# One overlapping request for x in both halves, earlier stores of a weight combination, and a new order in the first section and at the end

## The chip, the core and the metric

The kernel runs on one core of one Trainium2 chip. What counts is the device time of one execution in microseconds; the figure used is the median of several executions. TensorE (PE) multiplies, VectorE (DVE), ScalarE (ACT) and GpSimd (POOL) do the elementwise work, and SyncE (SP) issues the transfers (DMA) between the memory of the chip (DRAM) and the on-chip buffer of 128 partitions. Results of PE land in PSUM.

## What is computed

S = 2048 rows of D = 576 values; 32 heads of 18 values each; the feed-forward part has F = 4608 columns.

```python
def _A_ref(x, wqkv, wo):                      # attention, H = 32, Dh = 18
    qkv = (x @ wqkv).reshape(B, S, 3, H, Dh).transpose(2, 0, 3, 1, 4)
    ...
    p = softmax(einsum("bhqd,bhkd->bhqk", q, k) * (Dh ** -0.5))
    o = einsum("bhqk,bhkd->bhqd", p, v)
    return o.transpose(0, 2, 1, 3).reshape(B, S, D) @ wo

def _B_ref(x, w_gate, w_up, w_down):          # feed-forward
    return (gelu(x @ w_gate) * (x @ w_up)) @ w_down

xn = layernorm(x)
return x + _A_ref(xn, ...) * silu(_B_ref(xn, ...))
```

All of it is float32. The large products are made from high and low parts (hi = rounded, lo = raw - hi) in three terms: hi hi, lo hi, hi lo.

## The kernel before

**Stages.** The prologue normalises x, transposes it (x transposed, xn, called x below), splits it into a high part (xth) and a low part (xtl), stores both in the DRAM tensors xhs[b], one for each block b of TB = 512 rows, and makes Q, K and V. There a scheduler orders ACT, DVE and SP. Behind it PE's order is written out by hand: 144 sections of gate and up (4 blocks b, 18 row groups r of w_down, two sections g in each), between whose matmuls stand the matmuls of the attention, and after each two sections the product with w_down. At the end come the last sections and the projection of the attention's output, in 128-row groups, each called a step.

**A section** (section, gate_up) makes 128 columns of gate (pg) and of up (pu) for the 512 rows of the block. The 576 values of the contraction are 9 chunks of 64. Gate's chunk lies on the partitions 0 to 63, up's on 64 to 127, and the two matmuls of a pair run on the two halves of PE; a section has 27 pairs (9 chunks, three terms). So x has to lie in both halves: xd is three tiles (k = 0, 1, 2) of three chunks each, each with a high and a low tile, 128x3x512. The weights come by load_gu in two requests, one for each half (64x9x128 of w_gate, the same of w_up), and split_gu makes high parts (wh) and low parts (wl) of three chunks at a time. The weights of the next section are split in the section before: the first two thirds at its start, the last behind its pairs.

**The passage to the next block.** In the last section of a block (n + 1 divisible by 36) the x of the next block is loaded: load_xd hooks the tiles 0 and 1 behind the pairs 9 and 18 and loads tile 2 at the end. A request fills the partitions 0 to 63 only (halves = 1); copy_xd then copies the high tiles on ACT and the low tiles on POOL to the partitions 64 to 127. The tile 2 comes by two requests for each part instead (halves = 2). There are three passages, from block 0 to 1, 1 to 2 and 2 to 3; the first block's x (XD) is loaded in the prologue and copied by POOL.

**Attention between the pairs.** A slot makes scores (pm, max_pair) for the maximum on DVE, then scores (pe, score_pair), their exponential pT on ACT, and the values (acc). pm, pe, acc, py of w_down and the end's po share a ring of three PSUM slots (ring, RING = 3): PE waits where the reader of an older slot is late.

**w_down** (down) takes seven products of combined quarters of h (ah, al) and of the weights (T); DVE adds them into M. T is formed in the first blocks from raw rows (rawd; cut_plain_b, high_b, low_b) and for the groups in FORMED stored to the DRAM tensor ts (t_piece with store), to be loaded again later. The pieces of a group are stored at hooks, i.e. behind numbered pairs of the next section: 13 and 20 for the high pieces, 2 and 9 of the section after for the low.

**The end.** step() is one group of 128 rows: project (po from oh, ol and the output weights woh, wol), multiply (yy), between() (work put in here, as last_down), finish_rows (the sum into xx or xxs, and its store), and split_o(k + 2), which makes the high part oh on ACT and the low part ol on DVE of the group after the next. last_section makes the last gate and up sections, in PSUM of their own ("f") or in the ring ("ring"). ACT, DVE and POOL have the order of the program text here.

The line that fills the lower half, and the copy to the upper:

```python
nc.sync.dma_start(f(t)[HR * a:HR * a + HR],
                  xhs[b][i, k * XG * HR:(k + 1) * XG * HR, :].rearrange("(k p) t -> p k t", p=HR))
...
keep(nc.scalar.activation(x[0][HR:P, i], f(x[0])[0:HR, i], AF.Copy))
```

## Time and profile before

| what | before |
| --- | --- |
| median of three runs | 2551.31 us (2550.46 to 2553.19) |
| the profiled execution | 2552.37 us |
| its span | 2550.6 us |
| instructions | 52903 |
| granted TensorE clock | 1.00 |
| bytes moved, mean rate | 446.88 MB, 175 GB/s |
| ACT and POOL busy | 1461.7 us (57%), 1639.3 us (64%) |

The times are those of the device; the profile is of one execution, and its span leaves out what lies before the first and behind the last instruction. A row of the timeline reads: start in us from the span's start, duration in us, engine, line of the kernel, operation, output tile <- input tiles, shape, and how many instructions stand in the row; in brackets the idle time of the engine before it and the instruction that ended it. SPq is SP as the issuer of transfers, so that its duration is that of the issue and not of the transfer. PEld is the loading of weights into PE, which runs beside its matmuls.

### The profile page before, as it was taken

What the parts mean: (1) busy time and instruction counts of PE and PEld (TensorE: products, weight loads), DVE (VectorE), ACT (ScalarE), POOL (GpSimd) and SP (SyncE); (2) the same over time, 40 slices, a digit from 0 to 9 for tenths busy, and PEclk for the clock granted to TensorE, in tenths of its full rate; (3) what the DMA queues carried; (4) which work ended last, traced back from release to release, by engine and by line L of the source; (5) the groups of instructions that cost most, each with busy time, mean ns of one, the idle gap of its engine ahead of it and who ended that gap; (6) DMA issues with size and microseconds to landing.
All of it is one profiled execution on the core that took longest, in us unless ns stands there. A gap on an engine that the chain in (4) does not pass through costs nothing.

```text
span 2550.6 us, 52903 instructions
## 1 busy us (share of the span) xinstructions
PE 2537.9 (100%) x20548; PEld 1835.7 (72%) x20548; DVE 2092.3 (82%) x2371; ACT 1461.7 (57%) x1765; POOL 1639.3 (64%) x1708
## 2 busy tenths in 40 slices
PE   9999999999999999999999999999999999999999
PEld 8888866666766676666667666776666677666688
DVE  5327888889888888888887888998888888889367
ACT  3223466666666665555666555655556665556621
POOL 3105688888888875656658555666667666666773
PEclk9999999999999999999999999999999999999999
DMA  8855465555685566667787767766668666665775
GB/s 262 272 187 136 117 175 164 156 165 163 169 215 157 162 174 147 166 165 165 170 191 188 174 166 169 170 169 169 154 160 207 162 173 172 164 170 151 190 209 213
DMA packets 410321, 446.88 MB, mean 175 GB/s; under 512 B 107092, under 2 KB 287060, under 8 KB 410072
## 3 DMA queue, kind: packets, MB, share of 16 engines
q1 hardware_dynamic: 410072, 443.50, 65.7%
q8 instruction: 164, 2.69, 0.5%
q14 instruction: 85, 0.70, 0.1%
HBM read 347.30 MB, written 96.08 MB: 174 GB/s over the span
## 4 chain that ended last, share of the span: by engine, by line
PE 98%; DVE 1%; ACT 0%; DMA 0%; issue 0%; POOL 0%; SPq 0%; DVEq 0%
PE pg L431 24%; PE acc L887 18%; PE py L547 15%; PE pu L431 11%; PE pm L824 9%; PE pe L870 9%; PE po L200 6%; PE po L1041 2%; PE pgu L431 2%; PE py L534 1%; PE pt L270 0%; DVE KA L771 0%; DMA xx<-in_A_x_dram 0%; DMA KA<-qk 0%; ACT pT L871 0%
## 5 line engine op out<-in xcount | busy, mean ns | idle before, releaser
L871 ACT ACTIVATE pT<-pe 128x1024 f32<-128x1024 f32 x1024 | 1047.3, 1027 | 580.5 <-PE pe L870 547.6
L825 DVE TENSOR_REDUCE mx<-pm 128x2 f32<-128x1024 f32 x1024 | 1221.1, 1224 | 164.9 <-PE pm L824 148.3
L431 PE MATMUL pu<-xd,wh 64*128 64x512 f32 x2466 | 901.7, 396 | 0.0
L431 PE MATMUL pg<-xd,wh 64*128 64x512 f32 x2466 | 901.6, 396 | 0.0
L431 PEld LDWEIGHTS pg<-xd,wh 64*128 64x128 f32 x2466 | 454.6, 184 | 111.6 <-issue 53.9
L431 PE MATMUL pu<-xd,wl 64*128 64x512 f32 x1233 | 481.9, 391 | 0.0
L431 PE MATMUL pg<-xd,wl 64*128 64x512 f32 x1233 | 481.8, 391 | 0.0
L431 PEld LDWEIGHTS pu<-xd,wh 64*128 64x128 f32 x2466 | 454.6, 184 | 22.4 <-ACT xd L160 0.2
L887 PE MATMUL acc<-pT,VS 128*32 128x512 f32 x4096 | 466.0, 595 | 0.0
L117 POOL TENSOR_SCALAR wh<-raw 128x384 fp32r<-128x384 f32 x402 | 217.2, 542 | 370.4 <-PE pu L431 264.8
L119 POOL TENSOR_TENSOR wl<-raw,wh 128x384 fp32r<-128x384 f32 x402 | 415.8, 1036 | 28.4
L824 PE MATMUL pm<-KA,QT 64*128 64x512 f32 x2048 | 411.7, 394 | 3.0 <-ACT pT L871 2.7
L870 PE MATMUL pe<-QT,KA 64*128 64x512 f32 x2048 | 410.1, 392 | 0.0
L547 PE MATMUL py<-T,ah 128*128 128x288 f32 x1876 | 380.9, 298 | 0.0
L554 DVE TENSOR_TENSOR M<-py,M 128x576 f32<-128x576 f32 x448 | 339.4, 757 | 32.0 <-PE py L547 18.0
L547 PEld LDWEIGHTS py<-T,ah 128*128 128x128 f32 x1876 | 298.8, 188 | 54.0 <-issue 54.0
L460 POOL TENSOR_TENSOR al<-h,ah 128x512 fp32r<-128x512 f32 (+1 forms) x143 | 295.6, 2067 | 59.8 <-ACT ah L457 50.0
L887 PEld LDWEIGHTS acc<-pT,VS 128*32 128x32 f32 x4096 | 120.1, 109 | 276.6 <-issue 229.7
L547 PE MATMUL py<-T,al 128*128 128x288 f32 x938 | 276.1, 294 | 0.0
L870 PEld LDWEIGHTS pe<-QT,KA 64*128 64x128 f32 x2048 | 192.8, 184 | 109.4 <-DVE mx L825 24.3
L431 PEld LDWEIGHTS pg<-xd,wl 64*128 64x128 f32 x1233 | 227.4, 184 | 31.9 <-POOL wl L124 0.3
L431 PEld LDWEIGHTS pu<-xd,wl 64*128 64x128 f32 x1233 | 227.3, 184 | 11.9
(170 smaller groups left out, 2968.6 us busy)
## 6 DMA issues: line engine op xcount, KB each, us to landing
T<-ts SPq DMA_DIRECT2D x98, 576.0 KB
KA<-qk SPq DMA_DIRECT2D x768, 72.0 KB
T<-ts SPq DMA_DIRECT2D x98, 432.0 KB
raw<-in_B_w_gate_dram SPq DMA_DIRECT2D x144, 288.0 KB
raw<-in_B_w_up_dram SPq DMA_DIRECT2D x144, 288.0 KB
ts<-T SPq DMA_DIRECT2D x36, 576.0 KB
VS<-vs SPq DMA_DIRECT2D x128, 152.0 KB
qk<-t SPq DMA_DIRECT2D x72, 256.0 KB
```

Source lines behind the costliest of these rows:

```text
L117: first = nc.gpsimd.tensor_scalar(hi, raw, 1.0, 1.0, op0=ALU.mult, op1=ALU.mult)
L119: keep(nc.gpsimd.tensor_tensor(lo, raw, f(hi), op=ALU.subtract))
L200: nc.tensor.matmul(o, st, m, start=(i == 0), stop=(i == len(terms) - 1))
L431: nc.tensor.matmul(o, w[1 + wp][k][rr, c, :], xd[k][xp][rr, c, :], start=(i == 0), stop=(i == len(terms) - 1))
L460: low = two.tensor_tensor(lo, raw, f(hi), op=ALU.subtract)
L547: nc.tensor.matmul(py[:, t, 0:DC], h[:, i, tt], T[:, w, k], start=n == 0, stop=n == 2)
L554: nc.vector.tensor_tensor(M[:, m], py[:, :, 0:DC], M[:, m], op=ALU.add)
L824: nc.tensor.matmul(pm[:, a], QS[u, r][rr, t * P:(t + 1) * P], KS[(u * NA + c) % KB][r][rr, :], start=True, stop=True)
L825: nc.vector.tensor_reduce(MX[u][:, 2 * r:2 * r + 2, t, c], pm, axis=AX.X, op=ALU.max)
L870: nc.tensor.matmul(pe[:, a], KS[(u * NA + c) % KB][r][rr, t * P:(t + 1) * P], QS[u, r][rr, :], start=True, stop=True)
L871: nc.scalar.activation(PT[u, kt][:, 2 * r:2 * r + 2, :], pe, AF.Exp, scale=SCALE)
L887: nc.tensor.matmul(ACC[u][32 * a:32 * a + 32, :], VS[(u * NA + c) % VB][:, v:v + 32], pt[:, a, :], start=first, stop=last, skip_group_chec ...
```

## The change

Five things are changed.

1. xhs[b] has 64 more rows, a repetition of the first 64 of its block, written by two more stores in the prologue. load_xd makes one request of 128 partitions for each tile, in which partition p reads row 192 k + 64 c + p for c = 0, 1, 2: the partitions 64 to 127 read the rows that lie 64 further on. The upper half so holds each chunk's successor, and the copies on ACT and POOL are gone, those of the prologue too.
2. load_gu loads w_up shifted to match: chunks 1 to 8 in one request, chunk 0 in another at the end. A section has three weight requests in place of two.
3. The high pieces of the combination that is formed last before the passage from block 0 (`late`) are stored at the hooks 1 and 3 rather than 13 and 20.
4. In section 0, T's cut (cut_plain_b) stands behind the third split of the next weights.
5. At the end, step() splits o (split_o) before between() and finish_rows; the last section (first + 4) follows the section in the ring directly, its weights are loaded before the loads of T that follow, and split in two pieces ahead of the sums of h and one behind.

```diff
--- before.py
+++ after.py
@@ -105,7 +105,7 @@
     ys = dram.tile([S - TB, D], F32, name="ys")
     zeros = dram.tile([2, 2 * TB], F32, name="zeros")
     ts = dram.tile([NR, P, 2 * 7 * DC], F32, name="ts")
-    xhs = [dram.tile([2, D, TB], F32, name=f"xhs{b}") for b in range(NB)]
+    xhs = [dram.tile([2, D + HR, TB], F32, name=f"xhs{b}") for b in range(NB)]
 
     ident = const.tile([P, P], F32, name="ident")
     make_identity(nc, ident)
@@ -133,8 +133,9 @@
     def load_gu(t, keep=lambda i: i):
 
         raw = raw_tile([P, NC, P])
-        for a, w in enumerate((w_gate, w_up)):
-            keep(nc.sync.dma_start(raw[HR * a:HR * a + HR], w[:, t * P:(t + 1) * P].rearrange("(k p) n -> p k n", p=HR)))
+        cols = slice(t * P, (t + 1) * P)
+        for to, rows in ((raw[0:HR], w_gate[:, cols]), (raw[HR:P, 0:NC - 1], w_up[HR:D, cols]), (raw[HR:P, NC - 1:NC], w_up[0:HR, cols])):
+            keep(nc.sync.dma_start(to, rows.rearrange("(k p) n -> p k n", p=HR)))
         return raw, [], []
 
     def split_gu(w, k, cut=split):
@@ -143,24 +144,16 @@
         w[1].append(hi)
         w[2].append(lo)
 
-    def load_xd(b, k, halves=1):
+    def load_xd(b, k):
 
         out = []
         for i in range(2):
             t = wts.tile([P, XG, TB], F32R, name=f"xd{i}_{k}")
-            for a in range(halves):
-                nc.sync.dma_start(f(t)[HR * a:HR * a + HR],
-                                  xhs[b][i, k * XG * HR:(k + 1) * XG * HR, :].rearrange("(k p) t -> p k t", p=HR))
+            rows = xhs[b][i, k * XG * HR:(k + 1) * XG * HR, :].rearrange("(k p) t -> p k t", p=HR)
+            both = bass.AP(rows.tensor, rows.offset, [[rows.ap[0][0], P]] + [list(d) for d in rows.ap[1:]])
+            nc.sync.dma_start(f(t), both)
             out.append(t)
         return out
-
-    def copy_xd(x, part, keep=lambda i: i, i=slice(None)):
-
-        if part == 0:
-            keep(nc.scalar.activation(x[0][HR:P, i], f(x[0])[0:HR, i], AF.Copy))
-        else:
-            keep(nc.gpsimd.tensor_copy(x[1][HR:P, i], x[1][0:HR, i]))
-
 
     def after(what, before, reason):
         tc.add_manual_dep(what.ins, before.ins.name, mybir.DependencyInfo(
@@ -277,6 +270,7 @@
             for i in range(2):
                 keep(nc.sync.dma_start(xhs[b][i, 0:R0, :].rearrange("(k p) t -> p k t", p=P), f(xt[i])))
                 keep(nc.sync.dma_start(xhs[b][i, R0:D, :], f(xt[2])[HR * i:HR * i + HR, :]))
+                keep(nc.sync.dma_start(xhs[b][i, D:D + HR, :], f(xt[i])[0:HR, 0]))
 
         XT = [(pro.tile([P, KT, TB], F32R, name=f"xth{i}"), pro.tile([P, KT, TB], F32R, name=f"xtl{i}"),
                pro.tile([P, TB], F32R, name=f"xtr{i}")) for i in range(2)]
@@ -386,9 +380,6 @@
             nxt = transposes(b + 1, xr) if b + 1 < NB else None
             if b == 1:
                 XD = [load_xd(0, k) for k in range(NG)]
-                for xd in XD:
-                    for t in xd:
-                        nc.gpsimd.tensor_copy(t[HR:P], t[0:HR])
             if b == 2:
                 ahead = load_gu(0, tc.keep_in_program_order)
                 for k in range(NG):
@@ -603,7 +594,6 @@
                 split_gu(nxt, k, one)
         if n == 0:
             load_rawd(0)
-            hook(len(pairs) - 1, lambda: cut_plain_b(FF["rawd"]))
         if g == 0 and (b, r) in FORMED:
             raw = FF["rawd"]
             hook(12, lambda: sums_b(raw))
@@ -616,21 +606,16 @@
             p()
         if nxt:
             split_gu(nxt, NG - 1, one)
+        if n == 0:
+            cut_plain_b(FF["rawd"])
         FF["w"] = nxt
-        if new:
-            copy_xd(xd[0], 0, keep)
         FF["act"] = activate(pg, pu, g, n < ATT.stop)
         if g > 0 or n not in ATT:
             FF.pop("last", lambda: None)()
         if new:
-            xd.append(load_xd(b + 1, NG - 1, 2))
+            xd.append(load_xd(b + 1, NG - 1))
             for t in hooks.get(len(pairs), ()):
                 t()
-            for i in range(XG):
-                FF["hooks"].setdefault(2 + 2 * i, []).append(lambda i=i: copy_xd(xd[1], 0, keep, i))
-            for k in range(NG - 1):
-                for i in range(XG):
-                    copy_xd(xd[k], 1, keep, i)
             FF["xd"] = xd
 
     def downs(then={}):
@@ -652,6 +637,7 @@
         def behind(what):
             what(keep if (n + 1) % (NR * G) == 0 else lambda i: i)
 
+        late = (n + 2) % (NR * G) == 0 and n + 2 < NF
         if g == 1 and (b, r + 1) in NEXT:
             load_rawd(part(b, r + 1))
         if b == 0 and r < PLAIN:
@@ -670,7 +656,7 @@
                     high_b(1)
                 hook(9 if lead else 2, lambda: low_b(0))
                 hook(16 if lead else 10, lambda: low_b(1))
-                for k, i in enumerate((19, 24) if lead else (13, 20)):
+                for k, i in enumerate((19, 24) if lead else (1, 3) if late else (13, 20)):
                     hook(i, lambda k=k: t_piece(s, k, True))
                 sums_a(g, h, vec if lead else pool)
                 hook(12, lambda: cut_a(0, h, pool, pool, keep))
@@ -680,7 +666,6 @@
                 behind(lambda k: (sums_a(g, h, pool, k), cut_a(1, h, pool, pool, keep)))
         else:
             if g == 0:
-                late = (n + 2) % (NR * G) == 0 and n + 2 < NF
                 for k, i in enumerate((None, 5, 27, 27) if late else (None, 5, 13, 21)):
                     if i is None:
                         t_piece(s, k)
@@ -1064,13 +1049,13 @@
             po = project(k)
             if k < len(groups) - 1:
                 multiply(k, po, both)
+                split_o(k + 2)
                 between()
                 finish_rows(k, both)
             else:
                 for c in (slice(0, 1), slice(1, 2)):
                     multiply(k, po, c)
                     finish_rows(k, c)
-            split_o(k + 2)
             b, j = groups[k]
             if b < 2 and j == TB // P - 1:
                 load_o(b + 2)
@@ -1141,14 +1126,18 @@
         for k in range(2, 4):
             load_y(k)
         h1, gelu = last_section("f")
+        load_raw(first + 4)
         last_down(0)
         split_o(1)
         gelu()
+        last = FF["raw"].pop(first + 4)
+        for k in range(2):
+            split_gu(last, k)
         sums_a(0, h, pool)
         cut_a(0, h, pool, pool)
+        split_gu(last, 2)
         sums_a(1, h1, pool)
         cut_a(1, h1, pool, pool)
-        load_raw(first + 4)
         for i, u in enumerate(rest):
             store_scale(u, i)
         for m in ("rawd", "tsum"):
@@ -1159,18 +1148,19 @@
         for k in range(3):
             step()
         h, gelu = last_section("ring")
+        FF["w"] = last
+        h1, last_gelu = last_section("f")
+        gelu()
         step()
-        gelu()
+        last_gelu()
         step()
         step(lambda: last_down(1))
         sums_a(0, h, pool)
         cut_a(0, h, pool, pool)
-        h, gelu = last_section("f")
-        gelu()
-        sums_a(1, h, vec)
+        sums_a(1, h1, vec)
         M = FF["M"]
         step()
-        cut_a(1, h, act, pool)
+        cut_a(1, h1, act, pool)
         step()
         step(lambda: last_down(2, {0: ((pool, 5, ADD, 0), (pool, 5, ADD, 2)), 1: ((pool, 5, SUB, 1),)}))
```

On ACT the first passage is shown (pT are exponentials, h, t and accs the copies from PSUM, xd the copies of x). Before:

```order
L871 ACTIVATE pT<-pe 128x1024 x8
L160 ACTIVATE xd_0_8708<-xd_0_8708 64x1536
L440 ACTIVATE h_8805<-pg 128x512
L444 ACTIVATE t_8808<-pu 128x512
L446 ACTIVATE h_8805<-h_8805 128x512
L891 ACTIVATE accs<-acc 128x512
L871 ACTIVATE pT<-pe 128x1024
L160 ACTIVATE xd_1_8756<-xd_1_8756 64x512
L871 ACTIVATE pT<-pe 128x1024
L160 ACTIVATE xd_1_8756<-xd_1_8756 64x512 x2
L871 ACTIVATE pT<-pe 128x1024 x6
```

After the change:

```order
L856 ACTIVATE pT<-pe 128x1024 x8
L431 ACTIVATE h_8844<-pg 128x512
L435 ACTIVATE t_8847<-pu 128x512
L437 ACTIVATE h_8844<-h_8844 128x512
L876 ACTIVATE accs<-acc 128x512
L856 ACTIVATE pT<-pe 128x1024 x8
```

The four copies of xd are gone; the exponentials follow one another.

On SP the same passage (raw are weights, ts<-T the stores of the combination). Before:

```order
L152 DMA xd_0_8708<-xhs_79 64x3x512
L152 DMA xd_0_8710<-xhs_79 64x3x512
L489 DMA ts<-T 128x1152
L152 DMA xd_1_8756<-xhs_79 64x3x512
L152 DMA xd_1_8758<-xhs_79 64x3x512
L489 DMA ts<-T 128x864
L152 DMA xd_2_8813<-xhs_79 64x3x512 x2
L152 DMA xd_2_8816<-xhs_79 64x3x512 x2
```

After the change:

```order
L480 DMA ts<-T 128x1152
L480 DMA ts<-T 128x864
L154 DMA xd_0_8750<-xhs_79 128x3x512
L154 DMA xd_0_8752<-xhs_79 128x3x512
L154 DMA xd_1_8797<-xhs_79 128x3x512
L154 DMA xd_1_8799<-xhs_79 128x3x512
L154 DMA xd_2_8852<-xhs_79 128x3x512
L154 DMA xd_2_8854<-xhs_79 128x3x512
```

Both stores now stand ahead of all requests for x, and x comes by six requests of double the size.

On POOL the first sections (wl are low parts of weights, al of h, T of the w_down rows). Before:

```order
L124 TENSOR_TENSOR wl<-raw,wh 128x384 x2
L460 TENSOR_TENSOR T<-rawd,T 128x1152
L124 TENSOR_TENSOR wl<-raw,wh 128x384
L460 TENSOR_TENSOR al<-h_2034,ah 128x512
L124 TENSOR_TENSOR wl<-raw,wh 128x384 x3
```

After the change:

```order
L124 TENSOR_TENSOR wl<-raw,wh 128x384 x3
L451 TENSOR_TENSOR T<-rawd,T 128x1152
L451 TENSOR_TENSOR al<-h_2039,ah 128x512
L124 TENSOR_TENSOR wl<-raw,wh 128x384 x3
```

The third low part has passed T. On DVE, in each step of the end, the sum of finish_rows and the low part of split_o change places in the same way (`L1057 ... xxs<-xxs,yy` before `L1024 ... ol<-KA,oh`; now the other way round).

## The prediction

> **What bounds the kernel now.** I read the page's busy times and its chain first, then the waits of PE, and then cut the span into stretches that start where PE begins a product of w_down.
>
> ```profile
> PE 2537.9 (100%) x20548; PEld 1835.7 (72%) x20548; DVE 2092.3 (82%) x2371; ACT 1461.7 (57%) x1765; POOL 1639.3 (64%) x1708
> PE 98%; DVE 1%; ACT 0%; DMA 0%; issue 0%; POOL 0%; SPq 0%; DVEq 0%
> ```
>
> PE sets the time: of the span of 2550.6 us it is busy 2537.9, so all its gaps together are 12.7 us, the tail after its last matmul among them. The change removes no matmul; it can only win what PE loses by waiting. The waits of PE (us in all, times, longest):
>
> ```profile
> PE pm L824 <- ACT pT L871: 2.7, 4, 0.8
> PE po L1041 <- DVE ol L1024: 1.1, 2, 0.9
> PE pgu L431 <- POOL wl L124: 0.8, 1, 0.8
> ```
>
> These three are the ones that the change touches: score products that wait for ACT, the end's projections that wait for a low part, and one section that waits for the low part of its weights. A gap undercounts a stall, since a matmul's end is modelled and the pace before and after counts too. So I measure a stall by whole cycles. The next rows are stretches from the first w_down product of one pair of sections to that of the next (columns: window, length, busy PE, PEld, DVE, ACT, POOL, granted clock, DMA share, GB/s); the last one is an ordinary cycle, the first three hold the passage from one block of 512 rows to the next.
>
> ```profile
> 704.56:739.62 35.06, 34.19 (x283) 23.91 (x279) 29.16 (x30) 25.59 (x30) 25.59 (x28) 1.00 0.82 202
> 1305.12:1340.16 35.04, 34.13 (x282) 23.22 (x278) 28.96 (x30) 23.45 (x27) 21.03 (x25) 1.00 0.90 213
> 1905.84:1940.64 34.80, 33.91 (x282) 23.67 (x278) 29.32 (x31) 23.49 (x27) 19.45 (x23) 1.00 0.89 207
> 1706.18:1739.44 33.26, 33.26 (x282) 22.79 (x278) 29.02 (x31) 20.62 (x24) 21.82 (x23) 1.00 0.58 156
> ```
>
> With the same number of matmuls the passages cost 35.06 - 33.26 = 1.80, 1.78 and 1.54 us more: **5.1 us** together, while their gaps in the waits are 2.7. The granted clock is 1.00 everywhere, so nothing of this is throttle.
>
> **The passages, first part of the sum.** What ACT does in the first passage, and PE beside it:
>
> ```profile
> 720.76 1.48 ACT L160 ACTIVATE xd<-xd 64x1536 fp32r<-64x1536 f32 x1
> 726.19 0.63 ACT L160 ACTIVATE xd<-xd 64x512 fp32r<-64x512 f32 x1
> 726.84 1.02 ACT L871 ACTIVATE pT<-pe 128x1024 f32<-128x1024 f32 x1
> 727.89 1.15 ACT L160 ACTIVATE xd<-xd 64x512 fp32r<-64x512 f32 x2
> 729.07 1.94 ACT L871 ACTIVATE pT<-pe 128x1024 f32<-128x1024 f32 x2
> ```
>
> ```profile
> 724.09 0.50 PE L431 MATMUL pg<-xd,wh 64*128 64x512 f32 x1
> 724.31 0.49 PE L431 MATMUL pu<-xd,wh 64*128 64x512 f32 x1
> 724.43 0.60 PE L870 MATMUL pe<-QT,KA 64*128 64x512 f32 x2
> 727.92 0.50 PE L824 MATMUL pm<-KA,QT 64*128 64x512 f32 x2
> 728.96 0.39 PE L431 MATMUL pu<-xd,wh 64*128 64x512 f32 x1
> 730.14 0.50 PE L824 MATMUL pm<-KA,QT 64*128 64x512 f32 x2 [0.79 <-ACT pT L871]
> ```
>
> Here two losses are seen. ACT copies x into the upper half (1.48 + 0.63 + 1.15 = 3.26 us), three of these copies lie between exponentials, the exponential of 729.07 comes late, its PSUM slot frees late, and the score product of 730.14 waits 0.79 us. And gate and up, which start together in an ordinary section, run 724.31 - 724.09 = 0.22 us apart after the passage, since the up half's x exists only after a copy; the slots then pack worse (0.60 against the usual 0.40). The request of the change fills both halves at once and the copies are gone from ACT and from POOL (18 there, 0.61 us each by the row below), so both losses have lost their cause: -1.80 - 1.78 - 1.54 = **-5.1 us**. Should only the wait and its small forerunner go, a passage gives 730.14 - 728.96 = 1.18 less the ordinary step of 0.23, and some 0.25 for the smaller wait of the score product before it (at 727.92, where the step is 0.47), 1.2 us each, 3.6 in all.
>
> ```profile
> L162 POOL CAST xd<-xd x18: 604/610/1157, 719.9 to 1928.0; 64x512 fp32r<-64x512 f32 x18
> 720.17 2.57 SPq L152 DMA_DIRECT2D xd<-xhs  x4
> ```
>
> That holds only if x arrives as early as it did. The requests of before were 384 KB each to 64 partitions, eight of them in a passage; now six of 768 KB to 128. DMA rates, by windows: two while x came in (64 partitions), one while the end's KA came in (128 partitions):
>
> ```profile
> 716.50:718.50 2.00, 2.00 (x20) 1.57 (x18) 1.83 (x3) 1.61 (x2) 1.13 (x2) 1.00 1.10 207
> 721.00:723.00 2.00, 2.00 (x24) 0.63 (x20) 0.66 (x2) 1.97 (x3) 1.83 (x4) 1.00 1.05 203
> 2392.50:2394.00 1.50, 1.50 (x16) 1.23 (x14) 0.00 (x0) 1.43 (x3) 1.42 (x2) 1.00 1.04 397
> ```
>
> All three have the engines full (share over 1), so it is the target that makes the difference: 64 partitions take about 205 GB/s, 128 take 397. Thus 786 kB at 397 GB/s is 1.98 us, as long as 393 kB at 203 (1.94), and six requests take 11.9 us where eight took 15.5. The last tile is the first to be short: before, its four requests were issued at 720.17 to 722.74 behind four of 1.94 us; after, its two stand at the same place behind four of 1.98, and end earlier. In addition the two stores of the w_down combination (576 and 432 KB) now stand ahead of x rather than between its requests. They wait for their own data, not for x, and the hooks that hold x come 6 pairs later, so I take 0, with up to 1 us at each passage as the other bound (one x request's length, 1.98, half of it met by slack). If the doubled target did not double the rate, a request would take 3.9 us; that is the third rival.
>
> [...]
>
> **More requests everywhere.** w_up now comes in two requests, 144 added issues. In an ordinary section of before one takes SP:
>
> ```profile
> 1727.06 0.63 SPq L137 DMA_DIRECT2D raw<-in_B_w_up_dram  x1
> ```
>
> 144 x 0.63 = 91 us of SP over the run, 1.3 us in a cycle of 33.26 us. Nothing computes on SP; what is behind such an issue are K, Q and V loads of later slots, and in the ordinary cycle above DMA is busy 0.58 of the time. The bytes stay the same (8 + 1 chunks). I take 0; upper bound one issue in twenty shown to PE, 0.05 x 91 = 4.6 us.
>
> **First weights, second part.** Section 0 to 1, on PE and POOL:
>
> ```profile
> 207.69 0.39 PE L431 MATMUL pgu<-xd,wh 64*128 64x512 f32 x2
> 208.92 0.50 PE L431 MATMUL pgu<-xd,wl 64*128 64x512 f32 x2 [0.85 <-POOL wl L124]
> 204.77 2.69 POOL L460 TENSOR_TENSOR T<-rawd,T 128x1152 fp32r<-128x1152 f32 x1 [4.42 <-ACT T L457]
> 207.41 1.46 POOL L124 TENSOR_TENSOR wl<-raw,wh 128x384 fp32r<-128x384 f32 x1
> 208.82 1.29 POOL L460 TENSOR_TENSOR al<-h,ah 128x512 fp32r<-128x512 f32 x1
> 210.07 2.96 POOL L124 TENSOR_TENSOR wl<-raw,wh 128x384 fp32r<-128x384 f32 x3
> 211.14 0.50 PE L431 MATMUL pg<-xd,wl 64*128 64x512 f32 x1
> 204.59 0.51 ACT L123 ACTIVATE wh<-raw 128x384 fp32r<-128x384 f32 x1
> ```
>
> The low part of the last third stood behind the 2.69 us of T. Now it stands ahead, in the 4.42 us in which POOL waited for ACT's T. The step of PE there is 208.92 - 207.69 = 1.23 us against 0.23, so 1.0 us is freed. But the next section then wants its first low part 1.0 us sooner, at about 210.1 rather than 211.1, and that stands behind al: al waits for ACT's chain, which gains only some 0.4 us, the high part of 204.59 taken out of its way, so the first of the three is there at about 210.6 (210.07 + 2.96 / 3 = 211.06, less 0.4). The stall that goes there gives back 0.5. Net **-0.5 us**, bounds 0 and -1.0.
>
> **The end, third part.**
>
> ```profile
> 2529.49 0.29 PE L1041 MATMUL po<-wol,oh 128*128 128x288 f32 x1
> 2529.97 0.40 PE L1041 MATMUL po<-woh,ol 128*128 128x288 f32 x1 [0.19 <-DVE ol L1024]
> 2533.65 0.29 PE L1041 MATMUL po<-wol,oh 128*128 128x288 f32 x1
> 2534.83 0.40 PE L1041 MATMUL po<-woh,ol 128*128 128x288 f32 x1 [0.89 <-DVE ol L1024]
> 2533.41 0.76 DVE L1057 TENSOR_TENSOR xxs<-xxs,yy 128x576 f32<-128x576 f32 x1
> 2534.09 0.69 DVE L1024 TENSOR_TENSOR ol<-KA,oh 128x512 fp32r<-128x512 f32 x1
> ```
>
> The low part of the next group stood behind the sum of the finished rows; now it stands ahead of it and is 0.76 us earlier. The first stall, a step of 2529.97 - 2529.49 = 0.48 against 0.13, goes: 0.35. The second, 2534.83 - 2533.65 = 1.18, so 1.05 over 0.13, keeps what the 0.76 does not cover, and starts 0.35 earlier because the first is gone: 1.05 - 0.76 + 0.35 = 0.64 remain, so 0.4 is won. Together **-0.7 us**, bounds -0.35 (the first alone) and -1.4 (both). The gate section that moves forward in PE's order is 54 matmuls that are computed either way; PE has no stall where it stood, so it brings 0. What could be late through it, the M sums and the copy of al, has slack of over a microsecond: 0 as the middle, +0.5 as the bound.
>
> The sum: -5.1 - 0.5 - 0.7 = -6.3 us. The profiled execution took 2552.37 us (1.8 beside its span), 1.06 over the median of 2551.31; the terms belong to the program and not to the execution, so I take them off the median: **2545.0 us**, a ratio of 0.9975. This measurement can tell about 0.2% from no change, here 5.1 us, so the border of faster lies at 2546.2, only 1.2 above.
>
> **Rivals.** First, that only the named waits go and the rest of a passage's excess has another cause, the fuller DMA (share 0.82 to 0.90 against 0.58, which slows what it feeds): 3.6 + 0.35 + 0.5 = 4.4 us off, 2546.9; for it speaks that the gaps make up only half of the excess, against it the 0.22 us between gate and up, which is of the size of the rest. It ends within 0.2%. Second, that the change does not do what it says at the small places: the stall for the weights moves wholly to the next section and DVE stays late in the end; then 5.1 alone remain, 2546.2, on the border. Third, that the added issues and the new order of the splits on POOL (two high parts and then two low parts) show as 0.06 us in each of some 64 cycles: +3.8, 2548.8, unchanged. Fourth and slower: the source and not the target sets the rate of x. The overlapping rows are read twice, 768 KB at 205 GB/s is 3.8 us, the last tile lands some 6.5 us after PE wants it (issued from about 714 on, six times 3.9 is 737 to 739, wanted at 732), and three passages cost 3 x 6.5 - 5.1 = +14.4: about 2564 with the small gains off. It decides as soon as the rate is under about 260 GB/s (786 kB in 3.0 us, six from 714 to 732). For it speaks that no load of overlapping rows is in the trace; against it the 397 GB/s of a load of the same kind, 1024 KB to 128 partitions.
>
> **Chances.** The sum 0.52, the rivals 0.14, 0.12, 0.10 and 0.12, the fourth with whatever else could make a passage late. Faster by over 0.2%: the sum and half of the second, 0.58; within 0.2%: the first, the other half of the second, and the third, 0.30; slower: the fourth, 0.12. Range 2543.0 (passages 5.3, weights 1.0, end 1.4, and half a microsecond of run) to 2550.0 (the third rival with its bound). The likeliest case alone is 2544 to 2546.
>
> **What would show it.** Right: the three stretches at the passages last 33.3 us, with no wait of a score product for pT, gate and up starting together, and windows near 390 GB/s while x lands; no L160 or L162 on ACT and POOL; the ordinary cycles still 33.26; one wait of 0.5 behind al near 210, one of some 0.6 left in the end. Wrong: a wait of a section for x, ordinary cycles of 33.3 and more, or passages that stay over 34.

## The result, and the profile after

The changed kernel takes 2545.26 us (median of 8 runs, 2544.32 to 2547.46), the kernel before 2551.78 (8 runs) on the same chip: a ratio of 0.9975, 95% interval [0.9964, 0.9986], 6.5 us less where 6.3 were forecast (2545.0). A second series gave 2546.06 against 2552.09, again 0.9975 [0.9965, 0.9985]. The profiled execution took 2544.51 us with a span of 2542.7; against the one before it is 7.86 us shorter, more than the medians differ.

The page's busy times and chain, after the change:

```profile
PE 2534.6 (100%) x20548; PEld 1837.5 (72%) x20548; DVE 2092.2 (82%) x2371; ACT 1452.9 (57%) x1753; POOL 1620.2 (64%) x1684
PE 97%; DVE 1%; POOL 1%; issue 0%; DMA 0%; ACT 0%; SPq 0%; DVEq 0%; POOLq 0%
```

ACT has 12 instructions less and POOL 24, the copies; PE runs the same 20548 matmuls. The waits of PE that answer to those shown of before, and a new one:

```profile
PE pe L855 <- DVE mx L810: 0.3, 1, 0.3
PE po L1026 <- DVE ol L1009: 0.3, 1, 0.3
PE pm L809 <- ACT pT L856: 0.3, 1, 0.3
PE pg L422 <- POOL wl L124: 0.3, 1, 0.3
```

The waits for pT fell from 2.7 us to 0.3 (the one left is at the attention's start, away from the change), those for ol from 1.1 to 0.3, and the one for wl has moved from pgu to pg of the next section. New is a score product that waits for DVE's maxima. The cycles, cut as before at the first product of w_down (window, length, busy PE, PEld, DVE, ACT, POOL, granted clock, DMA share, GB/s): three passages, an ordinary cycle, and the cycle behind the first passage.

```profile
703.72:736.91 33.19, 33.19 (x282) 22.85 (x278) 28.81 (x30) 22.45 (x26) 22.76 (x23) 1.00 0.87 270
1302.68:1335.88 33.20, 33.20 (x283) 23.53 (x279) 28.99 (x31) 20.30 (x23) 17.09 (x18) 1.00 0.88 273
1901.28:1934.52 33.24, 33.24 (x282) 23.60 (x278) 28.85 (x30) 20.29 (x23) 16.04 (x17) 1.00 0.85 269
1701.48:1734.78 33.30, 33.30 (x283) 22.80 (x279) 28.90 (x31) 20.63 (x24) 21.89 (x23) 1.00 0.57 158
736.91:770.74 33.83, 33.52 (x282) 22.94 (x278) 30.53 (x34) 19.69 (x22) 33.18 (x32) 1.00 0.77 216
```

A passage is now as long as any other cycle, though DMA is as full as before (0.85 to 0.88). The first section behind the passage on PE, where gate and up start together and the slot behind them takes its usual 0.39 us:

```profile
723.20 0.50 PE L422 MATMUL pg<-xd,wh 64*128 64x512 f32 x1
723.20 0.49 PE L422 MATMUL pu<-xd,wh 64*128 64x512 f32 x1
723.53 0.39 PE L855 MATMUL pe<-QT,KA 64*128 64x512 f32 x2
```

And two windows of DMA while x comes in (207 and 203 GB/s in the windows shown of before):

```profile
719.00:721.00 2.00, 2.00 (x23) 0.69 (x24) 1.84 (x3) 1.82 (x3) 1.10 (x2) 1.00 1.05 400
721.00:723.00 2.00, 2.00 (x24) 0.46 (x16) 1.61 (x3) 0.63 (x1) 0.63 (x2) 1.00 1.06 393
```

Where the 7.86 us of the two profiled executions lie, from the starts of PE's groups (in us; "again" is the profiled execution of the second series):

| stretch | before | after | difference | again |
| --- | --- | --- | --- | --- |
| up to the first gate matmul | 197.35 | 197.19 | -0.16 | 196.84 |
| to the first product of w_down (first weights) | 20.86 | 20.12 | -0.74 | 19.98 |
| three passages | 104.91 | 99.63 | -5.28 | 99.68 |
| cycle behind the first passage | 33.24 | 33.83 | +0.59 | 34.27 |
| 54 ordinary cycles, sum | 1796.41 | 1795.84 | -0.57 | 1797.12 |
| the end: from 2430.39 (2424.07) to PE's last matmul | 115.56 | 113.88 | -1.68 | 113.93 |
| tail behind it | 4.64 | 4.77 | +0.13 | 4.77 |

The rest, -0.15, is spread over stretches that differ by 0.1. The sum over 54 cycles in which nothing was changed differs by 1.3 us between two executions of one kernel, so a table like this does not tell the total to better than a microsecond. A stretch in which nothing waits by chance repeats to 0.1 us, as the passages do in the last column. Others do not: in the profiles of the experiments below, the end took 115.56 to 116.41 us where nothing in it was changed, and the three passages 104.67 to 105.49 us where x came as before.

### The profile page after: what moved, and what is told of

The parts are those of the page before. It is cut to its first block, busy times and chain, and to the rows that moved or that the text cites. A ratio compares the mean times of both kernels' runs of the same rounds, so it can differ in the third digit from the quotient of the medians.

```text
span 2542.7 us, 53140 instructions
## 1 busy us (share of the span) xinstructions
PE 2534.6 (100%) x20548; PEld 1837.5 (72%) x20548; DVE 2092.2 (82%) x2371; ACT 1452.9 (57%) x1753; POOL 1620.2 (64%) x1684
## 4 chain that ended last, share of the span: by engine, by line
PE 97%; DVE 1%; POOL 1%; issue 0%; DMA 0%; ACT 0%; SPq 0%; DVEq 0%; POOLq 0%
PE pg L422 25%; PE acc L872 18%; PE py L538 15%; PE pm L809 9%; PE pe L855 9%; PE pu L422 9%; PE po L193 6%; PE po L1026 2%; PE pgu L422 2%; PE py L525 1%; PE pt L263 0%; POOL M L560 0%; DVE KA L756 0%; DMA xx<-in_A_x_dram 0%; DMA KA<-qk 0%
## 5 line engine op out<-in xcount | busy, mean ns | idle before, releaser
L117 POOL TENSOR_SCALAR wh<-raw 128x384 fp32r<-128x384 f32 x402 | 211.8, 530 | 456.8 <-PE pu L422 275.3
L119 POOL TENSOR_TENSOR wl<-raw,wh 128x384 fp32r<-128x384 f32 x402 | 422.4, 1054 | 26.4
```

The source lines that it names most:

```text
L117: first = nc.gpsimd.tensor_scalar(hi, raw, 1.0, 1.0, op0=ALU.mult, op1=ALU.mult)
L119: keep(nc.gpsimd.tensor_tensor(lo, raw, f(hi), op=ALU.subtract))
```

## The experiments

**The x part alone.** Of the change, only load_xd, load_gu, xhs and the copies; the stores of the combination stay at their old hooks 13 and 20, and the first section and the end are as before. Against the changed kernel, the line that decides here:

```diff
-                for k, i in enumerate((19, 24) if lead else (1, 3) if late else (13, 20)):
+                for k, i in enumerate((19, 24) if lead else (13, 20)):
```

> The kernel before with the x part of the change alone: the overlapping request, w_up shifted and in two requests, no copies; stores, first section and end as before. My theory: each of the three passages loses its whole excess, 33.2 to 33.3 us in place of 35.06, 35.04 and 34.80, so 5.1 to 5.3 us less in the trace and a ratio of 0.9980; the stores of the w_down combination between the x requests of the first passage cost nothing. The rival of the named waits alone (the fuller DMA causes the rest): passages of 33.8, 3.6 us less, 0.9986. The new wait of 0.3 us (a step of 0.71 for 0.23) some 58 us behind the first passage, seen at 762.08 after the change, comes here too if it belongs to the x part, by the order of POOL behind the passage.

Measured 2551.53 us against 2552.34, 0.9995 [0.9985, 1.0004]: hardly anything, where my theory wanted 0.9980. The second and third passage fell to 33.24 and 33.21 us, as forecast; the first rose to 36.84. The window of the first, and SP and PE in it:

```profile
704.00:740.84 36.84, 35.09 (x283) 24.14 (x279) 29.25 (x30) 22.55 (x26) 23.57 (x24) 0.95 0.79 253
713.07 0.91 SPq L154 DMA_DIRECT2D xd<-xhs  x2
714.07 0.44 SPq L480 DMA_DIRECT2D ts<-T  x1
716.32 1.55 SPq L154 DMA_DIRECT2D xd<-xhs  x2
717.96 0.62 SPq L480 DMA_DIRECT2D ts<-T  x1
719.55 0.91 SPq L154 DMA_DIRECT2D xd<-xhs  x2
733.01 0.50 PE L422 MATMUL pg<-xd,wh 64*128 64x512 f32 x1 [1.75 <-DMA xd<-xhs]
```

The stores of 576 and 432 KB stand between the requests for x, and the last tile comes 2 us late (PE idles 1.75, and the step is 2.18 us for 0.23). So the copies' cause holds in the second and third passage, and "the stores between cost nothing" does not: the x part needs the moved stores. The new wait behind the first passage is not named in this trace, but POOL has the changed kernel's order there, and the cycle takes 33.51 us for 33.24 before: the order comes with the x part.

**The stores at their old place in the changed kernel.**

```diff
-                for k, i in enumerate((19, 24) if lead else (1, 3) if late else (13, 20)):
+                for k, i in enumerate((19, 24) if lead else (13, 20)):
```

> The changed kernel with the two high stores of the last combination (576 and 432 KB) at their old hooks, between the requests for x of the first passage. My prediction took 0 for this edit: the first passage then stays at 33.2 us, and the kernel within 0.3 us of the changed one. The rival: the stores of 1008 KB push the last x request back by 1032 kB / 390 GB/s = 2.6 us, it lands past 731 and the first passage waits 0.5 to 2 us; the other two passages have no such stores and stay at 33.2.

Measured 2549.93 us against 2552.51, 0.9990 [0.9981, 1.0000]: of the 6 to 6.5 us of the whole change 2.6 are left. The first passage:

```profile
703.26:739.18 35.92, 33.75 (x283) 22.84 (x279) 28.96 (x30) 22.44 (x26) 22.38 (x23) 1.00 0.77 245
732.86 0.50 PE L422 MATMUL pg<-xd,wh 64*128 64x512 f32 x1 [2.08 <-DMA xd<-xhs]
```

That is 2.7 us over the changed kernel's 33.19, 2.1 of it the wait for x; the other two stay at 33.21. The two stores are 1032 kB, at 390 GB/s (385 to 400 in the changed kernel's windows from 719 to 727, where x came in) an estimated 2.6 us of DMA: the rival's sum. The profiled execution is the fastest of the ten (2547.88 us, the slowest 2551.61), so most of them lost more than this trace shows; where, no trace shows.

**ACT's copies put back, x still by the wide request.**

```diff
+    def again(x, keep, i=slice(None)):
+        keep(nc.scalar.activation(x[0][HR:P, i], f(x[0])[HR:P, i], AF.Copy))
...
+        if new:
+            again(xd[0], keep)
...
+            for i in range(XG):
+                FF["hooks"].setdefault(2 + 2 * i, []).append(lambda i=i: again(xd[1], keep, i))
```

> The changed kernel, with ACT's four copies per passage put back at their old places, each now a copy of the upper half onto itself (3.26 us per passage, values unchanged), while x still comes by the wide request. My theory: ACT's copies between the exponentials are the cause, so the passages go back to 34.4 to 35.1 us, 1.2 to 1.8 each, 3.6 to 5.4 us over the changed kernel; the wait of a score product for pT returns with about 0.8 us. The rival, that the fuller DMA or the late arrival of x made the passages long: they stay at 33.2 to 33.4, and the kernel stays within 1 us of the changed one.

Measured 2550.57 us, 0.9993 [0.9984, 1.0003]: some 5 us over the changed kernel. The three passages are 34.90, 34.90 and 34.67 us, and ACT and PE show what they showed before (first the window of the first passage):

```profile
703.99:738.89 34.90, 33.99 (x283) 23.33 (x279) 29.12 (x30) 25.60 (x30) 22.68 (x23) 1.00 0.81 258
727.28 1.15 ACT L159 ACTIVATE xd<-xd 64x512 fp32r<-64x512 f32 x2
723.49 0.50 PE L425 MATMUL pg<-xd,wh 64*128 64x512 f32 x1
723.70 0.49 PE L425 MATMUL pu<-xd,wh 64*128 64x512 f32 x1
729.53 0.50 PE L816 MATMUL pm<-KA,QT 64*128 64x512 f32 x2 [0.80 <-ACT pT L863]
```

Both losses are back, the wait of 0.80 us for pT and the 0.21 us between gate and up, with six wide requests and without POOL's copies. So ACT's 3.26 us of copies alone make 1.7, 1.7 and 1.4 us, almost all of a passage's excess; for the fuller DMA and POOL's copies together 0.1 to 0.2 us are left (35.06, 35.04 and 34.81 before), which single executions hardly tell from nothing.

**Two requests of 64 partitions for each tile.** The kernel before with halves = 2 everywhere and no copies:

```diff
-    def load_xd(b, k, halves=1):
+    def load_xd(b, k, halves=2):
...
-            copy_xd(xd[0], 0, keep)
```

> The kernel before, but every tile of x comes by two requests of 64 partitions, one for each half, with no copy on ACT or POOL: 12 requests of 393 kB in a passage. If only one request of 128 partitions reaches the double rate (my theory: half the partitions, half the rate, requests behind each other), a request takes 1.94 us, twelve 23 us, the last lands at about 739 where PE wants it at about 731: the passages lose their copies but wait for x, each 33.3 + 6 to 8 us, 39 to 41 us in place of 35, and the kernel is 10 to 18 us slower, a ratio of 1.004 to 1.007. If two requests to different halves run beside each other at the full rate, the passages take 33.3 us, as with the wide request, and the ratio is 0.998: then the width of one request is not what matters.

Measured 2574.94 us, 1.0086 [1.0071, 1.0101]. The passages take 43.78, 42.28 and 41.03 us, more than the 39 to 41 expected. The first passage, and DMA and PE in it (two windows, one row):

```profile
703.65:747.43 43.78, 38.34 (x282) 25.39 (x278) 29.06 (x30) 22.42 (x26) 22.52 (x23) 0.92 0.86 207
716.00:718.00 2.00, 2.00 (x20) 1.57 (x18) 2.00 (x2) 1.51 (x3) 1.92 (x3) 1.00 1.06 211
734.00:736.00 2.00, 1.55 (x8) 0.70 (x4) 1.23 (x1) 0.95 (x2) 0.00 (x0) 0.50 1.05 216
739.56 0.79 PE L428 MATMUL pu<-xd,wh 64*128 64x512 f32 x1 [1.12 <-DMA xd<-xhs]
```

Requests to the two halves are issued one behind the other, and the two windows shown move 211 and 216 GB/s; the changed kernel's two, with wide requests, move 400 and 393. Two other windows of the passage reach 352 (722 to 724) and 341 GB/s (730 to 732); what moved in them was not separated. So two half requests for each tile did not bring x in at the rate of one wide request: here it is the width of one request that doubles the rate. PE waits 12.9 us for x in this kernel (14 waits). This run also prices the rival in which x comes at half the rate: 23 us slower, not the 14.4 that I worked out for the passages. PE's granted clock falls behind the waits too (0.50 in the second window, 0.92 over the passage); how much of the difference that makes is not separated.

**Three weight requests a section, alone.**

```diff
-        for a, w in enumerate((w_gate, w_up)):
-            keep(nc.sync.dma_start(raw[HR * a:HR * a + HR], ...))
+        for to, rows in ((raw[0:HR], w_gate[:, cols]), (raw[HR:P, 0:NC - 1], w_up[0:D - HR, cols]), (raw[HR:P, NC - 1:NC], w_up[D - HR:D, cols])):
+            keep(nc.sync.dma_start(to, rows.rearrange("(k p) n -> p k n", p=HR)))
```

> The kernel before with w_up's weights in two requests (chunks 0 to 7 and chunk 8) and nothing else: 144 added issues on SP, 91 us of SP by 0.63 us each. My theory: they are hidden, ordinary cycles stay at 33.26 us, and the ratio is 1.000 within 0.0006. The rival: 0.06 us in each of 64 cycles, 3.8 us, a ratio of 1.0015, ordinary cycles of 33.32.

Measured 2552.56 us, 1.0002 [0.9993, 1.0012], and a median ordinary cycle of 33.25 us: the 144 issues are hidden in the ordinary cycles, and the 1.0015 of the rival lies outside the interval. In the profiled execution, the slowest of the ten, PE once waits for x in the second passage (0.26 us at 1334.19), which takes 35.68 us for 35.04; with the wide request this wait is not there (33.20).

**The end: both edits, and each alone.** The edit to step(), which is the whole of the third run and part of the first (the second has only the moved section):

```diff
                 multiply(k, po, both)
+                split_o(k + 2)
                 between()
                 finish_rows(k, both)
...
-            split_o(k + 2)
```

> The kernel before with the end's part alone, both the earlier low part and the moved gate section. From the trace of the changed kernel, where the end came out 1.7 us shorter: 1.6 to 1.8 us less between the last values of attention and PE's last matmul (121.8 us to 120.1 in the traces, 2424.19 to 2545.95 before), one wait for ol of 0.3 us left. By the sum of the prediction it would be 0.7. Ratio 0.9993 by the one, 0.9997 by the other.

> The kernel before with the gate section of the end moved ahead and its weights earlier, but the low part of o where it was (behind the sum of the rows). Theory now: the surplus of the end's gain over the 0.7 predicted comes from this move, because the two gate sections run as one of 108 matmuls (12.46 us against 6.37 + 6.36) and one change of PE between kinds of matmul is gone: 0.4 to 0.6 us less, and both waits for ol (0.19 and 0.89 us of gap) stay. The rival: the move brings 0 as predicted, and the whole surplus comes from the earlier low part; then the end is as long as before within 0.1 us.

> The kernel before with the earlier low part of o alone (split_o ahead of between() and finish_rows), the gate section where it was. The prediction's replay: the first wait for ol goes (0.35 us), the second keeps 0.64 us of 1.05, so the end is 0.7 us shorter than 115.56 us (from the last pair of sections that was measured, 2430.39, to PE's last matmul), 114.8. The rival, which the moved section's loss without this edit suggests (117.19): the two edits need each other, and this one alone brings more, 1.0 or above, while the section alone costs 1.6.

| kernel | time, ratio | from 2430.39 us (of before) or the same matmul to PE's last |
| --- | --- | --- |
| before | 2552.51, 1 | 115.56 |
| both edits | 2550.86, 0.9993 [0.9984, 1.0003] | 114.30 |
| section alone | 2552.15, 0.9999 [0.9990, 1.0008] | 117.19 |
| earlier low part alone | 2550.63, 0.9995 [0.9986, 1.0005] | 114.71 |
| whole change | 2545.26, 0.9975 [0.9964, 0.9986] | 113.88 |

The times tell none of them from 1; the stretch does. The earlier low part alone gives 0.85 us, near the 0.7 of the replay, but made up otherwise: the last projections, where both stalls stood, take 26.68 us for 27.72, 1.04 less, with 0.46 us of the second stall left and not 0.64, while a group of w_down products before them takes 6.01 us for 5.67. The section alone costs 1.6 in this execution. The waits of PE in that kernel:

```profile
PE po L1041 <- DVE ol L1024: 1.9, 4, 0.9
PE py L547 <- DVE yy L1049: 0.6, 1, 0.6
```

Four waits for ol where there were two, and one of a w_down product for the multiplication. The latter, some 0.7 us of the 1.6, also stands once in the kernel with three requests and in the one with two half requests, whose ends are unchanged and took 116.41 and 116.21 us, so it may be chance. The two added waits for ol stand in none of the five other profiles with the old step(), but this kernel too was profiled only once. With the low part early these go, except for the last, and the section's own gain is left: the two gate sections run as one group of 108 matmuls in 12.46 us where they took 6.37 and 6.36, 0.27 us less, and the groups around them are 0.1 us shorter each. So the edits do not add up: +0.9 to +1.6 and -0.85 alone, -1.3 together, and -1.7 in the whole change, in both of its profiled executions. Of the last difference, 0.35 us is one small wait for ol at 2509 that the one kernel has and the other has not; why is not settled.

**The first section alone.**

```diff
-            hook(len(pairs) - 1, lambda: cut_plain_b(FF["rawd"]))
...
+        if n == 0:
+            cut_plain_b(FF["rawd"])
```

> The kernel before with the order of the first section alone: T's cut behind the third split of the next weights. The step of 1.23 us at 208.92 goes, a step of 0.6 to 0.7 appears one section later at about 210.2 behind al, and the first product of w_down starts 0.5 to 0.8 us earlier than at 218.22. If the start-up differs by chance, the length from the first gate matmul (197.35) to that product says it: 20.87 us before, 20.1 to 20.4 here. Ratio 0.9997, not to be told from 1 by time alone.

Measured 2552.50 us, 1.0001 [0.9991, 1.0010], and 20.02 us from the first gate matmul to the first product of w_down, as expected. But the kernels without this edit have the same length: 20.15 (three requests), 20.10 (end), 19.93 (section), 19.88 (low part), 20.22 (x part), 20.32 (two halves). The 20.86 of the profile before was that execution's. In it ACT cut T 6.17 us behind the first gate matmul (203.52 less 197.35), released by a DMA; in the other kernels it is 5.1 to 5.6. With the old order and T in time (the section's run):

```profile
203.60 2.69 POOL L460 TENSOR_TENSOR T<-rawd,T 128x1152 fp32r<-128x1152 f32 x1 [3.45 <-PE pg L431]
206.25 1.47 POOL L124 TENSOR_TENSOR wl<-raw,wh 128x384 fp32r<-128x384 f32 x1
```

Counted from the first gate matmul, wl starts 1.0 us sooner than in the profile before (9.09 us behind it for 10.06), and PE does not wait for it. The edit should make the start safe against a late landing, though no profile with it has one; in the usual execution it brings under 0.1 us.

**The new wait, and a try to remove it.** Behind the first passage of the changed kernel, POOL, DVE and PE:

```profile
755.02 1.42 POOL L117 TENSOR_SCALAR wh<-raw 128x384 fp32r<-128x384 f32 x2
756.41 1.99 POOL L119 TENSOR_TENSOR wl<-raw,wh 128x384 fp32r<-128x384 f32 x2
758.36 1.29 POOL L462 TENSOR_TENSOR h<-h,h 128x512 f32<-128x512 f32 x1
760.45 0.22 POOL L820 TENSOR_TENSOR m<-nm,m 128x16 fp32r<-128x16 f32 x1
760.71 0.21 DVE L825 STREAM_TRANSPOSE mt<-m 128x32 f32<-128x32 f32 x1 [0.45 <-POOL m L820]
762.08 0.50 PE L855 MATMUL pe<-QT,KA 64*128 64x512 f32 x2 [0.31 <-DVE mx L810]
```

POOL splits two thirds of the next section's weights (3.4 us) before the sums of h and m; before the change they stood behind the cut of h. DVE's transposition waits for m, the maxima behind it are late, and PE loses 0.6 us (1.0 in the other profiled execution of this kernel). The wait stands at this place in four profiles (both of the changed kernel, and those with ACT's copies back and with the stores at their old place), but its size is chance's in part (gaps of 0.31 to 0.74 us), and single waits of the kind, of 0.56 and 0.60 us, also stand near 1765 in the kernels with the end's edits and with three requests, where x comes as before. Two kernels tried to win this back, the second with two more edits:

```diff
-            keep(nc.gpsimd.tensor_copy(m2[:, :, 0], n2))
-            keep(nc.gpsimd.tensor_tensor(m2[:, :, 1], n2, f(m2)[:, :, 0], op=SUB))
+            keep(nc.vector.tensor_copy(m2[:, :, 0], n2))
+            keep(nc.vector.tensor_tensor(m2[:, :, 1], n2, f(m2)[:, :, 0], op=SUB))
...
-            cut_plain(g, h)
+            cut_plain(g, h, vec if n == 0 else pool)
...
+                if k >= 9:
+                    split_o(k + 2)
                 multiply(k, po, both)
-                split_o(k + 2)
+                if k < 9:
+                    split_o(k + 2)
```

> The changed kernel with the two small operations that split the negated maxima (m from nm, 0.20 and 0.22 us) on DVE in place of POOL. Theory: the wait of 0.3 us at 762.08 (a cycle of 33.83 for 33.25) comes because POOL, behind the splits of the weights and the sums of h, makes m late, DVE's transposition stands 0.45 us for it and the maxima behind it are late. Then the cycle behind the first passage falls to 33.25, no score product waits for DVE's mx anywhere, and the other cycles stay at 33.25 because DVE has 4 us to spare in each; 0.6 us less, 2544.7. The rival: DVE's maxima are late for their own work, the wait stays, and the added 0.4 us per unit on DVE show in ordinary cycles: 33.3 or more, 2546 to 2548.

> The changed kernel with the maxima on DVE, the low part of the first h (al of section 0) on DVE in place of POOL, and in the end's steps from the tenth on the split of o ahead of the multiplication too. Theory: besides the 0.6 us behind the first passage, the wait of 0.27 us at 210.22 goes (a step of 0.66 for 0.23), since wl stands on POOL no longer behind al, 0.43; and the wait for ol at 2526.83 goes (a step of 0.58 for 0.13), 0.45, since ol is 0.68 us earlier: 1.5 us less than the changed kernel, about 2543.8, and the end 113.4 us in place of 113.88. The rival: what is won at the small places turns up as the next wait behind it, and the kernel stays within 0.5 us of the changed one.

Measured 2573.51 us, 1.0082 [1.0068, 1.0096], and 2573.38 us, 1.0081 [1.0067, 1.0095]: 27 us over the changed kernel, far beyond the rival. The cycle behind the first passage did fall to 33.21 us, so m on POOL was its cause. But PE pays in 28 other cycles, behind DVE. DVE, POOL and PE in the first of them, and the wait summed:

```profile
357.96 1.23 DVE L819 CAST m<-nm 128x16 fp32r<-128x16 f32 x1
359.22 0.66 DVE L820 TENSOR_TENSOR m<-nm,m 128x16 fp32r<-128x16 f32 x1
357.87 1.28 POOL L462 TENSOR_TENSOR h<-h,h 128x512 f32<-128x512 f32 x1 [1.37 <-DVE h L439]
360.53 0.50 PE L855 MATMUL pe<-QT,KA 64*128 64x512 f32 x2 [0.60 <-DVE accs L878]
PE pe L855 <- DVE accs L878: 20.2, 28, 1.5
```

The cast of 16 values a row takes 1.23 us, ending where POOL's sum of h ends (359.15). Of the 32 casts, 31 overlap an instruction of POOL and end within 0.04 us of the end of one; the other, at 287.32 with POOL idle, takes 0.17 us. The 28 waits lie in 28 cycles, just those that take over 33.9 us. The two other edits of the second kernel did what was expected: 19.55 us from the first gate matmul to w_down's first product (20.12 and 19.98 in the two executions of the changed kernel), no wait for ol, and an end of 113.39 us (113.88). Together they are worth some 0.9 us; a kernel with these two and without the maxima on DVE was not run.

**The changed kernel once more.**

> The changed kernel once more, unaltered, beside the others on the same chip. Both theories: 2545.3 within 0.7 us, passages of 33.2 us, end of 113.9 us; the sum of the 54 ordinary cycles 1795.8 within 1 us says how much one execution differs from the next where nothing is changed.

Measured 2546.06 us, 0.9975 [0.9965, 0.9985]; passages of 33.23, 33.26 and 33.19 us, end 113.93. The sum of the ordinary cycles was 1797.12, 1.3 over, a little more than expected.

## Why the prediction was right, point by point

- **The passages** (-5.1 us): 5.28 in one execution, 5.23 in the other. That ACT's copies are the cause, both of the late exponential and of the 0.22 us between gate and up, is shown by putting them back. The rival "only the named waits go" is refuted by the same run and by the passages of 33.2 us at a DMA share of 0.87.
- **x in time** (a request of 786 kB in 1.98 us): 393 to 400 GB/s against 397 taken from KA's load. The rival of the slow source did not come; its price was too low, as two half requests show: 23 us in place of 14.4.
- **The moved stores** (0, up to 1 us of cost at each passage): here the step failed, though not the sum. It compared six requests with eight and took the stores as a possible cost of the new place. They are what x would have waited for at the old one: 2.7 us in the first passage. The 11.9 us for six requests held only because the 2.6 us of stores were out of the way. That they had to be is shown by two runs; in the kernel before, the same stores stood between the requests and the passage's time was set by the copies.
- **More requests** (0): shown for the ordinary cycles by the run with them alone.
- **First weights** (-0.5 us): in the trace 0.74, but the term was mis-sized: a stall of 1.0 us read from one execution, which six other kernels with the old order do not show at that size (19.88 to 20.32 us against 20.86). That the profile after came out 0.74 us shorter, near the forecast, is luck: the execution profiled before happened to have the stall. Its usual worth is under 0.1 us. The forecast that a stall goes to the next section, behind al, came true (a gap of 0.27 us at 210.22, a step of 0.66 for 0.23, so 0.43 where 0.5 was said).
- **The end** (-0.7 us): 1.68. The low part's share came out near its size, 0.85 alone, through two errors that cancel (1.04 in the last projections, less 0.34 by a longer w_down group that may be chance); the moved section was put at 0, as a move with no stall to remove. It costs 0.9 to 1.6 alone and gains some 0.4 to 0.8 behind the other edit.
- **Not foreseen**: the wait of 0.6 to 1.0 us behind the first passage, from an order of POOL that came with the x part (the run with that part alone has it too).

So the measured total, 6.0 to 6.5 us less, is made of -5.3 for the passages, -1.7 for the end, under -0.1 for the weights and +0.6 to +1.0 for the new wait. The largest term was right in size and cause; that the total fell within 0.3 us of the forecast is luck, since the errors of the small terms have opposite signs.

## What to carry to other kernels

Copies on an engine that is idle 43% of the time cost the bound engine about half their length here (1.4 to 1.7 us in a passage for 3.26 us of copies), because they stood between the links of a chain of exponentials; one request over all partitions, whose rate doubled with the width (393 to 400 GB/s for 203 to 207), fills both halves in the time that one took (1.98 us for 1.94, estimates from 397 and 203 GB/s). When transfers are made to arrive just in time, count everything that shares their queue, stores too: here two of them, 1032 kB, cost the first passage 2.7 us. A stall that stands in one profile at a place where a transfer lands should be looked for in a second execution before it gets a term.

## What was not expected of the hardware

After the wait of 1.75 us for x in the kernel with the x part alone, the granted clock fell. Two windows behind it (columns as above), and then one behind the wait of 2.08 us of the kernel with the stores at their old place:

```profile
733.00:735.00 2.00, 1.99 (x13) 1.60 (x15) 0.62 (x1) 1.02 (x1) 0.00 (x0) 0.73 0.49 101
735.00:737.00 2.00, 2.00 (x12) 1.35 (x8) 0.67 (x2) 1.02 (x1) 0.00 (x0) 0.50 0.84 199
```

```profile
735.00:737.00 2.00, 2.00 (x22) 0.69 (x24) 1.84 (x3) 1.81 (x3) 0.00 (x0) 1.00 0.95 229
```

In the first kernel 12 matmuls in place of 22 are begun in 2 us at a clock of 0.50, and the passage is 3.6 us too long for a wait of 1.75; in the second the longer wait left the clock at 1.00 and cost 2.7. So the wait of 1.75 us cost about twice its length and the longer one 1.3 times its own: in these two cases the length does not say when the clock falls. What makes it fall, no trace shows.

The other is the cast above: 0.17 us beside an idle POOL and up to 1.24 us (median 1.22) beside a working one, where it ends within 0.04 us of the end of an instruction of POOL. What holds it until then the rows do not show. On POOL the 32 casts of the changed kernel take 0.19 to 0.21 us. So this small operation, moved from POOL to DVE, cost up to six times its size there.
